# Keys and values of batches 1 and 2 laid five tokens to a partition: a cosformer attention and SwiGLU kernel on one core

## The chip, the cores and the metric

The kernel runs on one core of a Trainium2 chip. The metric is the device time of one execution in microseconds, as a median of several runs; smaller is better. A separate profiled execution gives a trace of every engine: TensorE (PE, with its weight loads shown as PEld), VectorE (DVE), ScalarE (ACT), GpSimd (POOL) and SyncE (SP, which only issues transfers). Times in the trace are counted from the start of the span.

## The reference, cut to what matters

```python
B, H, S, D = 8, 8, 576, 64                      # attention, float32
theta = pi / 2 * arange(S) / S
phi(x) = concat([relu(x) * cos(theta), relu(x) * sin(theta)], -1)     # 128 features
kv  = einsum('bhsf,bhsd->bhfd', phi(k), v)      # 128 x 64 for each head
z   = sum(phi(k), axis=2)
num = einsum('bhsf,bhfd->bhsd', phi(q), kv)
den = einsum('bhsf,bhf->bhs', phi(q), z)[..., None] + 1e-6
x   = (num / den) with heads joined             # 4608 tokens x 512
# then for every token: x / rms(x) * rms_g, and
out = (silu(xn @ w_gate) * (xn @ w_val)) @ w_out     # 512 -> 1536 -> 512
```

The sum over the 576 tokens of a head may be taken in any order. So the tokens of k and v may lie on the partitions in any way, as long as k, v and the cos and sin tables agree.

## The kernel before, in words

Most of the work is the feed-forward part: for each block of 512 tokens (one batch less its last 64 tokens; block 8 collects those tails) 12 steps `gval_step` of two products of 512x512 with 128 output features each, and then 4 steps `out_step`. The attention of the next batch is spread over these steps. Nothing is scheduled automatically: the order of the source is the order on each engine, and a table `slots` (filled by `at(block, step, where, function, ...)`, run by `run`) says in which step which small piece of attention is issued. For block 0 there is a separate opening, written out by hand (`unit_mm`, `unit_tile`, `unit_silu`, `unit_h`, and between them `nd0_pe`, `nd_post`, `x_sq`, `x_norm`, `x_tr_pe`, `x_tr_evac`).

For each batch, k and v are loaded as float32 (`load_kv`) into one of five `raw` buffers. `k_phi` (L292 on ACT, L294 on DVE) multiplies k by the cos or sin column of its token and takes the positive part, into the bfloat16 tile `kp`; `v_cast` copies v to bfloat16 with a column of ones behind each head, so that one product gives kv and z. `kvz_pe` does these products into `psA`, and `kvz_evac` copies the result out.

There are two layouts of k and v. In the narrow one (batches 0, 1 and 2) a pair of heads shares the 128 partitions, 64 each, with nine consecutive tokens of a head on each partition: 9 steps of `k_phi` with 4 x 64 elements on 128 partitions, and 9 x 8 products over 64 rows each. In the wide one (batches 3 to 7) a partition holds five consecutive tokens of all eight heads, and 116 partitions are in use: 5 steps of `k_phi` with 8 x 64 elements, and 5 x 8 products over 116 or 115 rows (the last partition holds one token). The narrow load is one transfer; the wide load is two, of 112 and of 4 partitions (L115). Batch 0 has its own code for most of this.

The loads of batches 0 to 2 and of all weights are issued by GpSimd's queue, those of batches 3 to 7 by SP's. GpSimd works in order, and besides issuing it runs small operations: the power -0.5 that ends the RMS (`rs`, L520, inside `x_sq`), which `x_norm` on VectorE reads, two `q_phi` and one `v_cast`. In the program, the transfers of GpSimd signal their ends on eight semaphores that are taken in turn, one semaphore for each transfer. GpSimd's transfers in the order of the source are, by number:

1 q of batch 0, first half (L135); 2 and 3 v of batch 0 (L213); 4 q of batch 0, second half; 5, 6, 7, 8 `wg`, `wv`, `wg`, `wv`, first eight feature blocks (L183); 9 k of batch 1 (L110); 10 `wg`, last four blocks; 11 `wv`, last four blocks; 12 q of batch 1 (L126); 13 v of batch 1 (L110); 14, 15, 16 `wo` in three parts (L189); 17 k of batch 2; 18 v of batch 2.

The part of the opening in which these lie reads, shortened:

```python
    x_sq(0, 1)
    load_q(1, eng=G)
    load_kv("v", 1, eng=G)
    ...
    x_sq(0, 2)
    load_wo(0, 4)
    ...
    x_sq(0, 3)
    load_wo(4, 8)
    load_wo(8, 12)
    unit_silu(1)
    x_norm(0, 3)
    unit_mm(2, wg)
    x_tr_pe(0, 2, psC[1])
    ...
```

with `x_tr_pe(0, 3)` after six of the eight products of `unit_mm(3, wg)`. Here `x_sq(0, j)` issues a square on ScalarE and then `rs` on GpSimd.

Of the kernel before, what the change touches and what calls it, by code (L numbers as in the profile page):

```python
# [10 lines left out]
BF16 = mybir.dt.bfloat16  # L11
# [6 lines left out]
def kernel(  # L18
# [11 lines left out]
    nc = tc.nc  # L30
    B, H, S, D = q.shape
    DM = H * D
    DFF = moe_w_gate.shape[1]
    P = 128
    TB = 512
    HP = H // 2
    NC = S // 64
    NC5 = 5
    KP = S // NC5 + 1
# [3 lines left out]
    E = D + 1  # L43
# [3 lines left out]
    V, A, G = nc.vector, nc.scalar, nc.gpsimd  # L47

    ctx.enter_context(tc.manual_schedule())
    one = ctx.enter_context(tc.tile_pool(name="one", bufs=1))  # L50
# [22 lines left out]
        )  # L73

    def wide(b):
        return b > 2

    def rows_of(c):
        return KP if c == 0 else KP - 1
# [12 lines left out]
    def raw_tile(which, b):  # L92
        if (which, b) not in raw:
            t = ring.tile([P, H * NC5 * D], FP32, name="raw", tag="raw")
            raw[(which, b)] = t
        return raw[(which, b)]

    def raw_kv(which, b):
        t = raw_tile(which, b)
        if wide(b):  # L100
            return t[:, :].rearrange("p (h e) -> p h e", h=H)
        return t[:, 0 : HP * NC * D].rearrange("p (hp e) -> p hp e", hp=HP)
# [4 lines left out]
    def load_kv(which, b, hps=(0, HP), eng=nc.sync):  # L107
        src = k if which == "k" else v
        if not wide(b):
            return eng.dma_start(  # L110
                out=raw_kv(which, b)[:, hps[0] : hps[1], :], in_=kv_rows(src, b, hps)
            )
        last = KP if b < B - 1 else KP - 1
        for r0, r1 in ((0, KM), (KM, last)):
            eng.dma_start(  # L115
                out=raw_kv(which, b)[r0:r1, :, :], in_=kv_rows5(src, b, r0, r1)
            )
        if last < KP:
            eng.dma_start(
                out=raw_kv(which, b)[last:KP, :, :].rearrange("p h (c d) -> p h c d", d=D),  # L120
                in_=src[b, :, S - 1 : S, :].rearrange("h s d -> s h d").unsqueeze(2)
                .to_broadcast([1, H, NC5, D]),
            )
# [98 lines left out]
    part, left = [], 1e-6  # L222
# [42 lines left out]
    def cos_of(c):  # L265
# [3 lines left out]
    kp = kp5[:, :, :, :].rearrange("p c h f -> p (c h f)")[:, 0 : NC * HP * F].rearrange(  # L269
        "p (c hp f) -> p c hp f", c=NC, f=F  # L270
    )
    vv = one.tile([P, HP, NC, E], BF16, name="vv")
    vv5 = one.tile([P, H, NC5, E], BF16, name="vv5")
    G.memset(vv[:, :, :, D:E], 1.0)
    G.memset(vv5[:, :, :, D:E], 1.0)
    qpT = one.tile([P, H, TB], BF16, name="qpT")
    xnT = [one.tile([P, NDT, TB], BF16, name=f"xnT{i}") for i in range(2)]
# [6 lines left out]
    def copy(eng, o, i):  # L284
        if eng is A:
            A.copy(out=o, in_=i)  # L286
        else:
            eng.tensor_copy(out=o, in_=i)  # L288

    def phi(eng, out_ap, in_ap, scale):  # L290
        if eng is A:
            A.activation(out=out_ap, in_=in_ap, func=AF.Relu, scale=scale)  # L292
        else:
            eng.tensor_scalar(  # L294
                out=out_ap, in0=in_ap, scalar1=scale, scalar2=0.0, op0=ALU.mult, op1=ALU.max
            )


    def k_phi(eng, b, c, part, hps=(0, HP)):
        o = slice(0, D) if part == 0 else slice(D, F)  # L300
        f = cos_of if part == 0 else sin_of
        if wide(b):
            rows = rows_of(c)
            src = raw_kv("k", b)[0:rows, :, c * D : (c + 1) * D]
            phi(eng, kp5[0:rows, c, :, o], src, f(14 + c)[0:rows, :])
            return
        src = raw_kv("k", b)[:, hps[0] : hps[1], c * D : (c + 1) * D]
        phi(eng, kp[:, c, hps[0] : hps[1], o], src, f(c))

    qp_tiles = {}  # L310

# [55 lines left out]
        copy(eng, qpT[:, :, j * P : (j + 1) * P], dst)  # L367

    def v_cast(eng, b, hps=(0, HP)):
        if wide(b):  # L370
            src = raw_kv("v", b).rearrange("p h (c d) -> p h c d", d=D)
            hs = slice(2 * hps[0], 2 * hps[1])
            return copy(eng, vv5[0:KP, hs, :, 0:D], src[0:KP, hs])
        copy(
            eng, vv[:, hps[0] : hps[1], :, 0:D],
            raw_kv("v", b)[:, hps[0] : hps[1], :].rearrange("p hp (c d) -> p hp c d", d=D),
        )

    heads = psA[:, :, 0 : HP * E].rearrange("p g (hp e) -> p g hp e", e=E)
    kvzs = {}  # L380

    def kvz_pe(b):
        for hp in range(HP):
            for c in range(NC5 if wide(b) else 0):
                for g in range(2):
                    h, r = 2 * hp + g, rows_of(c)
                    nc.tensor.matmul(  # L387
                        heads[:, g, hp, :], lhsT=kp5[0:r, c, h, :], rhs=vv5[0:r, h, c, :],
                        start=(c == 0), stop=(c == NC5 - 1),
                    )  # L390
            for c in range(0 if wide(b) else NC):
                for g in range(2):
                    lo, hi = 64 * g, 64 * g + 64
                    nc.tensor.matmul(  # L394
                        heads[:, g, hp, :], lhsT=kp[lo:hi, c, hp, :], rhs=vv[lo:hi, hp, c, :],
                        start=(c == 0), stop=(c == NC - 1),
                    )


# [211 lines left out]
    for c in range(NC):  # L611
        k_phi(V, 0, c, 0)
        k_phi(A if c < 8 else V, 0, c, 1)
        z0_pe(c)
        if c < NDT:
            g_spread(psC[0], c)
# [65 lines left out]
    lo, hi = (0, NDT // 2), (NDT // 2, NDT)  # L682
# [75 lines left out]
    def at(blk, n, where, f, *args):  # L758
        slots.setdefault((blk, n), {}).setdefault(where, []).append((f, args))
# [2 lines left out]
        for f, args in slots.get((blk, n), {}).get(where, []):  # L762
            f(*args)

    KCS = ((0, 1, 2), (3, 4), (5, 6), (7, 8))
    KCS5 = ((0, 1), (2,), (3,), (4,))
    for c in range(NC):
        at(0, 5 + c // 3, "post", k_phi, V, 1, c, 0)
        at(0, 5 + c // 3, "post", k_phi, A, 1, c, 1)
    for j in range(4):  # L770
        at(0, (8, 8, 9, 10)[j], "post", q_phi, V, 1, j, 0)
        at(0, 8 + j, "post", q_phi, A, 1, j, 1)
# [2 lines left out]
        at(0, 10 + j, "pre" if j < 2 else "pe", q_tr_evac, V if j < 2 else A, 1, j, bank)  # L775
    at(0, 8, "post", load_kv, "k", 2, (0, HP), G)
    at(0, 9, "post", v_cast, G, 1, (0, 2))
    at(0, 10, "post", v_cast, V, 1, (2, 4))
    at(0, 10, "post", load_kv, "v", 2, (0, HP), G)
    at(0, 12, "pe", kvz_pe, 1)  # L780
    at(0, 12, "pe", kvz_evac, A, 1)

# [21 lines left out]
    for nb in range(2, B):  # L804
        b = nb - 1
        first = nb == 2
        for i, cs in enumerate(KCS5 if wide(nb) else KCS):
            kb, kn = ((0, 14), (0, 15), (1, 0), (1, 1))[i] if first else (b - 1, 12 + i)
            for c in cs:
                at(kb, kn, "post", k_phi, V, nb, c, 0)  # L810
                at(kb, kn, "post", k_phi, A, nb, c, 1)
        for i in range(2):
            vb, vn = ((0, 15), (1, 0))[i] if first else (b - 1, 13 + 2 * i)
            at(vb, vn, "post", v_cast, V, nb, (2 * i, 2 * i + 2))
        for j in range(4):
            late = j + (nb == 3)
            qb, qn = (b, 1 + j) if first else (b - (late < 2), (14 + late) % 16)
            at(qb, qn, "post", q_phi, V, nb, j, 0)
            at(qb, qn, "post", q_phi, A, nb, j, 1)
            at(qb, qn, "post", q_tr_dma, nb, j)  # L820
        kz = 3 if first else 2
        at(b, kz, "pe", kvz_pe, nb)
        at(b, kz, "pre", kvz_evac, A, nb)
        for j in range(4):
            n = ((6, 8, 9, 11) if first else (4, 6, 8, 10))[j]
            at(b, n, "pe", nd_pe, nb, j)
            at(b, n, "pre", nd_post, nb, j)
            at(b, n, "post", x_sq, nb, j)
            m = n + 2 if first and j == 0 else n + 1
            at(b, m, "post", x_norm, nb, j)  # L830
            at(b, m, "post", x_tr_dma, nb, j)

    for pair in range(4):
        b = 2 * pair or 3
# [9 lines left out]
    for nb in range(3, B):  # L844
        b = nb - 2
# [94 lines left out]
```

## Time and profile before

| | |
|---|---|
| median of 3 runs | 323.63 us (323.45 to 323.72) |
| the profiled execution, its own time | 323.16 us |
| its span | 321.4 us |
| granted TensorE clock, mean over the span | 0.999 |
| busy PE, DVE, ACT, POOL | 317.2, 184.5, 166.2, 40.4 us |
| loads of k and v by GpSimd | 2 and 2 transfers of 1152.0 KB |
| loads of k and v by SP | 5 and 5 of 1120.0 KB, with 4 and 4 of 40.0 KB, 1 and 1 of 30.0 KB, 1 and 1 of 10.0 KB |

A group of instructions in the profile is named by line, engine, operation, the tile written and the tiles read, with the shape and the number of them. In a timeline a row gives the start, the time, the engine and line, and in brackets the idle time of the engine ahead of it with what ended it. "us to landing" of a transfer counts from its issue to the end of its last packet.

### The profile page before, as it was taken

To read this page: it belongs to the slowest core of one execution; us is meant where nothing else is said; L and a number is where in the kernel's file an instruction comes from. 1 tells how busy PE (TensorE), PEld (TensorE's weight loads), DVE (VectorE), ACT (ScalarE), POOL (GpSimd) and SP (SyncE) were. 2 spreads that over 40 slices of the span, in tenths; PEclk is the share of its full clock that TensorE was granted. 3 is DMA by queue.
4 is the path that set the end of the run, shared out by engine and by line. 5 is a ranking of instruction groups with operands and counts; after the bars stand their busy time and mean duration, and the time that the engine had idled before them with its cause. 6 is when DMAs were issued, how large, how long until landed. Compare 5 with 4: busy or idle time off the path is not lost.

```text
span 321.4 us, 6061 instructions
## 1 busy us (share of the span) xinstructions
PE 317.2 (99%) x2310; PEld 162.5 (51%) x2310; DVE 184.5 (57%) x382; ACT 166.2 (52%) x322; POOL 40.4 (13%) x79
## 2 busy tenths in 40 slices
PE   8999999999999999999999999999999999999996
PEld 2689564554454445444544445544544444444444
DVE  7976858668447773777457645781676034204410
ACT  5766756754584466554744575446543333223321
POOL 9771211002001100011001100100011000000000
PEclk9999999999999999999999999999999999999999
DMA  7999999987999989999799859995522500041002
GB/s 234 238 274 268 279 330 159 262 183 189 227 224 203 194 260 189 234 250 168 159 190 230 195 161 200 198 217 162 99 58 42 116 33 0 0 102 31 1 35 98
DMA packets 80091, 53.76 MB, mean 167 GB/s; under 512 B 52234, under 2 KB 74046, under 8 KB 80062
## 3 DMA queue, kind: packets, MB, share of 16 engines
q1 hardware_dynamic: 73110, 41.25, 62.0%
q0 software_dynamic: 6944, 12.13, 15.5%
q8 instruction: 18, 0.29, 0.4%
q14 instruction: 11, 0.09, 0.1%
q10 hardware_dynamic: 8, 0.00, 0.0%
HBM read 37.83 MB, written 9.44 MB: 147 GB/s over the span
## 4 chain that ended last, share of the span: by engine, by line
PE 97%; DVE 1%; ACT 0%; issue 0%; POOL 0%; ACTq 0%
PE psC L579 27%; PE psG L556 27%; PE psV L556 27%; PE psA L449 2%; PE psV L648 2%; PE psG L579 2%; PE psG L648 2%; PE psA L387 2%; PE psC L603 1%; PE psC L410 1%; PE psA L394 1%; PE psA L474 0%; PE psV L363 0%; PE psG L430 0%; PE psC L546 0%; PE psC L233 0%
## 5 line engine op out<-in xcount | busy, mean ns | idle before, releaser
L576 DVE TENSOR_TENSOR hT<-psV,sg 128x512 bf16<-128x512 f32 x100 | 68.9, 689 | 97.7 <-PE psV L556 65.4
L575 ACT ACTIVATE sg<-psG 128x512 f32<-128x512 f32 x100 | 59.2, 592 | 62.3 <-PE psG L556 61.0
L556 PE MATMUL psV<-xnT,wv 128*128 128x512 bf16 x352 | 90.3, 379 | 0.0
L556 PE MATMUL psG<-xnT,wg 128*128 128x512 bf16 x352 | 90.3, 379 | 0.0
L579 PE MATMUL psC<-wo,hT 128*128 128x512 bf16 (+1 forms) x408 | 88.9, 376 | 0.0
L579 PEld LDWEIGHTS <-hT 128*128 128x128 bf16 x456 | 43.0, 98 | 47.8
L556 PEld LDWEIGHTS <-wv 128*128 128x128 bf16 x400 | 39.1, 98 | 47.2
L556 PEld LDWEIGHTS <-wg 128*128 128x128 bf16 x400 | 36.9, 98 | 39.8 <-DVE xnT L288 0.4
L520 POOL TENSOR_TENSOR rs<-ms,mhalf 128x1 f32<-128x1 f32 x36 | 20.5, 571 | 194.6 <-ACT scr L515 194.4
L286 ACT COPY osb<-psC 128x512 f32<-128x512 f32 x32 | 18.8, 586 | 49.9 <-PE psC L579 49.9
L515 ACT ACTIVATE scr<-xt 128x513 bf16<-128x513 f32 x36 | 22.8, 634 | 25.1 <-DVE xt L499 24.4
L527 DVE SCALAR_TENSOR_TENSOR xn<-xt,rs,gb 128x512 bf16<-128x512 f32 (+1 forms) x37 | 27.0, 731 | 9.9 <-POOL rs L520 9.8
L292 ACT ACTIVATE kp<-raw,tab 128x256 bf16<-128x256 f32 (+2 forms) x51 | 28.8, 607 | 2.2 <-DMA raw<-in_k_dram 2.2
L499 DVE TENSOR_TENSOR xt<-psA,rec 128x512 f32<-128x512 f32 x36 | 24.9, 691 | 1.2
L292 ACT ACTIVATE qp<-raw,tab 128x512 bf16<-128x512 f32 (+1 forms) x36 | 23.4, 666 | 1.0 <-DMA raw<-in_q_dram 0.8
L294 DVE TENSOR_SCALAR kp<-raw,tab 128x256 bf16<-128x256 f32 (+2 forms) x53 | 19.9, 423 | 0.5 <-DMA raw<-in_k_dram 0.5
L294 DVE TENSOR_SCALAR qp<-raw,tab 128x512 bf16<-128x512 f32 (+1 forms) x34 | 15.4, 466 | 4.2 <-DMA raw<-in_q_dram 4.2
L449 PEld LDWEIGHTS <-qpT 128*128 128x128 bf16 x224 | 10.5, 97 | 6.7 <-issue 0.7
L556 PE MATMUL psV<-xnT_tail,wv 128*128 128x512 bf16 x48 | 12.3, 379 | 0.0
L556 PE MATMUL psG<-xnT_tail,wg 128*128 128x512 bf16 x48 | 12.3, 379 | 0.0
L449 PE MATMUL psA<-kvzs,qpT 128*128 128x65 bf16 x224 | 11.4, 193 | 0.0
L288 DVE CAST vv<-raw 116x1280 bf16<-116x1280 f32 (+1 forms) x13 | 10.5, 807 | 1.1 <-DMA raw<-in_v_dram 1.1
(100 smaller groups left out, 178.2 us busy)
## 6 DMA issues: line engine op xcount, KB each, us to landing
out_dram<-osb SPq DMA_DIRECT2D x27, 256.0 KB, 2.3
raw<-in_q_dram SPq DMA_DIRECT2D x6, 1024.0 KB, 9.3
raw<-in_k_dram SPq DMA_DIRECT2D x5, 1120.0 KB, 8.5
raw<-in_v_dram SPq DMA_DIRECT2D x5, 1120.0 KB, 9.5
raw<-in_k_dram POOLq DMA_DIRECT2D x2, 1152.0 KB, 19.4
raw<-in_v_dram POOLq DMA_DIRECT2D x2, 1152.0 KB, 16.0
out_dram<-osb SPq DMA_DIRECT2D x17, 128.0 KB, 2.7
wg<-in_moe_w_gate_dram POOLq DMA_DIRECT2D x3, 512.0 KB, 13.6
```

The costliest lines, as they stand in the source:

```text
L286: A.copy(out=o, in_=i)
L292: A.activation(out=out_ap, in_=in_ap, func=AF.Relu, scale=scale)
L294: eng.tensor_scalar(out=out_ap, in0=in_ap, scalar1=scale, scalar2=0.0, op0=ALU.mult, op1=ALU.max)
L449: nc.tensor.matmul(heads[:, g, hp, :], lhsT=qpT[:, h, j * P : (j + 1) * P], rhs=kvzs[b][:, g, hp * E : (hp + 1) * E], start=True, stop=True,)
L499: V.tensor_tensor(out=xt[:, 0:DM].rearrange("p (hp g d) -> p g hp d", g=2, d=D), in0=heads[:, :, :, 0:D], in1=rec[:, :, :].unsqueeze(3).to ...
L515: A.activation(out=scr[:, :], in_=xt[:, 0 : DM + 1], func=AF.Square, scale=1.0 / math.sqrt(DM), accum_out=ms[:, :],)
L520: G.tensor_tensor(out=rs[:, :], in0=ms[:, :], in1=mhalf[:, :], op=ALU.pow)
L527: V.scalar_tensor_tensor(out=xn_of[(b, j)][:, c], in0=x_of[(b, j)][:, c], scalar=rs_of[(b, j)][:, :], in1=gb[:, c], op0=ALU.mult, op1=ALU. ...
L556: nc.tensor.matmul(bank[:, cols[0] : cols[1]], lhsT=w[:, t, n * P : (n + 1) * P], rhs=x[:, t, cols[0] : cols[1]], start=(t == 0), stop=(t ...
L575: A.activation(out=sg[:, :], in_=g[:, 0:TB], func=AF.Silu)
L576: V.tensor_tensor(out=hT[:, n, :], in0=v[:, 0:TB], in1=sg[:, :], op=ALU.mult)
L579: nc.tensor.matmul(bank[:, 0 : cols[1] - cols[0]], lhsT=hT[:, n, j * P : (j + 1) * P], rhs=wo[:, n, cols[0] : cols[1]], start=(n == 0), st ...
```

## The change

Batches 1 and 2 take the wide layout too: `wide(b)` is true from batch 1 on. With it the tile `vv` of the narrow layout and its memset go, and so do the narrow branches of `v_cast` and `kvz_pe`; the steps of `k_phi` of batch 1 in block 0 and of batch 2 become five instead of nine. `load_kv` for batches 1 and 2 issues two transfers on GpSimd's queue where it issued one, at the same places in the source. The order of everything else stays.

```diff
     def wide(b):
-        return b > 2
+        return b > 0
...
-    vv = one.tile([P, HP, NC, E], BF16, name="vv")
     vv5 = one.tile([P, H, NC5, E], BF16, name="vv5")
-    G.memset(vv[:, :, :, D:E], 1.0)
...
-        src = raw_kv("k", b)[:, hps[0] : hps[1], c * D : (c + 1) * D]
-        phi(eng, kp[:, c, hps[0] : hps[1], o], src, f(c))
+        phi(eng, kp[:, c, :, o], raw_kv("k", b)[:, :, c * D : (c + 1) * D], f(c))
...
     def v_cast(eng, b, hps=(0, HP)):
-        if wide(b):
-            src = raw_kv("v", b).rearrange("p h (c d) -> p h c d", d=D)
-            hs = slice(2 * hps[0], 2 * hps[1])
-            return copy(eng, vv5[0:KP, hs, :, 0:D], src[0:KP, hs])
-        copy(
-            eng, vv[:, hps[0] : hps[1], :, 0:D],
-            raw_kv("v", b)[:, hps[0] : hps[1], :].rearrange("p hp (c d) -> p hp c d", d=D),
-        )
+        src = raw_kv("v", b).rearrange("p h (c d) -> p h c d", d=D)
+        hs = slice(2 * hps[0], 2 * hps[1])
+        copy(eng, vv5[0:KP, hs, :, 0:D], src[0:KP, hs])
...
-            for c in range(NC5 if wide(b) else 0):
+            for c in range(NC5):
...
-            for c in range(0 if wide(b) else NC):
-                for g in range(2):
-                    lo, hi = 64 * g, 64 * g + 64
-                    nc.tensor.matmul(
-                        heads[:, g, hp, :], lhsT=kp[lo:hi, c, hp, :], rhs=vv[lo:hi, hp, c, :],
-                        start=(c == 0), stop=(c == NC - 1),
-                    )
...
-    KCS = ((0, 1, 2), (3, 4), (5, 6), (7, 8))
     KCS5 = ((0, 1), (2,), (3,), (4,))
-    for c in range(NC):
-        at(0, 5 + c // 3, "post", k_phi, V, 1, c, 0)
-        at(0, 5 + c // 3, "post", k_phi, A, 1, c, 1)
+    for c in range(NC5):
+        at(0, 5 + c // 2, "post", k_phi, V, 1, c, 0)
+        at(0, 5 + c // 2, "post", k_phi, A, 1, c, 1)
...
-        for i, cs in enumerate(KCS5 if wide(nb) else KCS):
+        for i, cs in enumerate(KCS5):
```

More of the change, by code (lines that the diff above doesn't have):

```diff
@@ L296, in phi, with k_phi @@
             )
-    def k_phi(eng, b, c, part, hps=(0, HP)):
+    def k_phi(eng, b, c, part):
         o = slice(0, D) if part == 0 else slice(D, F)
```

## The prediction

> **What bounds the kernel now.** I read the page first, its busy times and the chain that ended last.
>
> ```profile
> PE 317.2 (99%) x2310; PEld 162.5 (51%) x2310; DVE 184.5 (57%) x382; ACT 166.2 (52%) x322; POOL 40.4 (13%) x79
> ...
> PE 97%; DVE 1%; ACT 0%; issue 0%; POOL 0%; ACTq 0%
> ```
>
> TensorE sets the end: 97% of the chain is products, one behind the other. So an edit counts only if it changes the products or makes TensorE wait. The chain in order of time has the products that change, as pieces (start, length):
>
> ```profile
> 59.58 1.27 PE psA L394 x72
> ...
> 91.36 1.23 PE psA L387 x40
> ```
>
> L394 is the narrow form, L387 the wide one. The 72 products over 64 rows cost hardly more than 40 over 116, so their count promises nothing.
>
> What else the change touches is GpSimd's queue, so next I read its timeline around the loads.
>
> ```profile
> 15.73 0.82 POOL L183 DMA_DIRECT2D wv<-in_moe_w_val_dram  x1
> 16.68 0.56 POOL L520 TENSOR_TENSOR rs<-ms,mhalf 128x1 f32<-128x1 f32 x1
> 17.21 0.94 POOL L126 DMA_DIRECT2D raw<-in_q_dram  x1
> 18.15 0.77 POOL L110 DMA_DIRECT2D raw<-in_v_dram  x1
> 19.80 0.56 POOL L520 TENSOR_TENSOR rs<-ms,mhalf 128x1 f32<-128x1 f32 x1 [0.89 <-ACT scr L515]
> 20.32 0.79 POOL L189 DMA_DIRECT2D wo<-in_moe_w_out_dram  x1
> 21.56 0.56 POOL L520 TENSOR_TENSOR rs<-ms,mhalf 128x1 f32<-128x1 f32 x1 [0.45 <-ACT scr L515]
> 22.09 0.79 POOL L189 DMA_DIRECT2D wo<-in_moe_w_out_dram  x1
> 23.47 0.74 POOL L189 DMA_DIRECT2D wo<-in_moe_w_out_dram  x1 [0.60 <-DMA wv<-in_moe_w_val_dram]
> 26.69 0.76 POOL L110 DMA_DIRECT2D raw<-in_k_dram  x1 [2.48 <-DMA raw<-in_k_dram]
> ```
>
> Two rows matter. The third wo load waits for a wv load whose data it does not touch, and k of batch 2 waits for k of batch 1, whose buffer is another one. By number they are transfer 16, which waits for 8, and 17, which waits for 9: a transfer waits until the one eight before it has landed, for its semaphore. The landing times of 7 (issued 6.65), 8 (7.45) and 9 (8.97), each the last number of its row:
>
> ```profile
> wg<-in_moe_w_gate_dram POOLq DMA_DIRECT2D x1, 512.0 KB, 13.6
> ...
> wv<-in_moe_w_val_dram POOLq DMA_DIRECT2D x1, 512.0 KB, 15.7
> ...
> raw<-in_k_dram POOLq DMA_DIRECT2D x1, 1152.0 KB, 17.2
> ```
>
> They land at 20.25, 23.15 and 26.17, and the waits above end at 23.47 and 26.69, 0.32 and 0.52 later. Before the change, both waits stand behind the last rs of the opening, so nobody waits for them.
>
> Last, who reads rs: VectorE's norm, then TensorE's transposes.
>
> ```profile
> 20.55 0.74 DVE L527 SCALAR_TENSOR_TENSOR xn<-xt,rs,gb 128x512 bf16<-128x512 f32 x1
> 22.16 0.75 DVE L527 SCALAR_TENSOR_TENSOR xn<-xt,rs,gb 128x512 bf16<-128x512 f32 x1 [0.87 <-POOL rs L520]
> ```
>
> ```profile
> 22.18 0.39 PE L546 MATMUL psC<-ident,xn 128*128 128x128 bf16 x4
> 22.40 0.82 PE L648 MATMUL psG<-xnT,wg 128*128 128x256 bf16 x6
> 23.05 0.39 PE L546 MATMUL psC<-ident,xn 128*128 128x128 bf16 x4
> ```
>
> The norm of tile 3 ends at 22.91 and its transposes run at 23.05: rs of tile 3 has almost no slack to TensorE.
>
> **The change part by part.**
>
> *Products.* Twice 1.27 us becomes twice 1.23: 0.08 us saved on the path.
>
> *ScalarE, VectorE, casts.* k of batch 1 costs ACT three pieces of 1.29 and DVE three of 0.87 (3.87 and 2.61). Batch 3, wide, costs ACT 1.33 and three of 0.72, DVE 1.27 and 0.88 (3.49 and 2.15). A half of the v cast goes from 0.74 to 0.83 on DVE; GpSimd's half, 1.15 for 1152 columns, to about 1.28 for 1280 by size. All of it lies beside products: nothing on the path. One memset (0.27) leaves GpSimd.
>
> *Transfers, time of the data.* A load becomes 928 runs of 1280 B in place of 512 of 2304 B, with 1160 KB for 1152. In the queue's order wv lands at 31.0, q of batch 1 at 34.1 (1024 runs of 1024 B in 3.1 us) and v at 37.05 (512 of 2304 B in 2.95). Over 16 DMA engines that is 48 and 92 ns a run, by a line 57 ns for 1280 B: an estimate of 58 x 57 ns = 3.3 us, 0.35 more. If the four last rows run on four engines only, 8 more runs, 0.45 us, come on top. Bounds: 0 (bytes alone) to 0.8 us a load; I take 0.4, nearest the line. Who would feel it: q of batch 1 has 0.8 us (its first ACT step ends at 34.88, the transposes start at 35.70) against one load; k and v of batch 2 have 3.7 and 4.2 us (landed 48.3 and 51.25, used at 51.99 and 55.45) against four. The tightest is the second wo part, landed at 42.1 and used at about 42.7, with two loads ahead of it: 0.6 us of cover against 0.8. Bare, that would cost 0.2 us (0 to 1.0); with TensorE later by the next step it costs nothing.
>
> *Transfers, their issue.* Four more issues of about 0.76 us, and every number behind them moves. The new count: 9 and 10 k of batch 1, 11 wg, 12 wv, 13 q, 14 and 15 v of batch 1, 16 to 18 wo, 19 and 20, 21 and 22 the loads of batch 2. Then:
>
> - 10 waits for 2 (landed 9.5), 11 for 3 (3.75 + 7.3 = 11.05): GpSimd issues wg at about 11.35, its memset ends near 12.5, and its two q steps start at 12.68 as before, since that is when ACT releases them (1.62 us idle there).
> - 15, the four rows of v, waits for 7 (20.25): issue at 20.57, end at 21.31. Queued behind it is rs of tile 2, which moves from 19.80 to 21.31.
> - 16, the first wo part, waits for 8 (23.15), as transfer 16 does now: it starts at the same 23.47 and ends at 24.21. Queued behind it is rs of tile 3, which moves from 21.56 to 24.21: 2.65 us.
>
> VectorE's norm of tile 3 started 0.60 after rs did, so it starts at 24.81 and ends at 25.56; the transposes of tile 3 go from 23.05 to about 25.7. Those of tile 2, pushed from 22.18 to 22.7, are inside this. On VectorE the norm is ahead of the copy of tile 2's transposes and of the first two products with silu, and all go along. What follows needs TensorE's own results; the largest of the later waits of TensorE's weight loads is 0.43 us, at 54.21, for a tile made on this same chain. So I see nothing to take the 2.65 back. Later issues (17 waits for 9, 18 for 10, 19 for 11, 20 for 12) keep GpSimd busy waiting until about 32, with transfers queued for the DMA engines all that time and no rs before 45.72. Bounds for the step: release 0.1 to 0.5 (0.32 as seen), issue 0.7 to 0.94: 2.35 to 3.05.
>
> *Sum.* 323.16, the profiled execution's own time (span 321.4 and 1.76 around it), less 0.08, plus 2.65, gives 325.73. The median of the runs stands 0.47 above that execution: 326.2. With the bounds, 325.7 to 326.8.
>
> **The rivals.**
>
> *The clock drops in the gap.* TensorE would idle from about 23.5 to 25.7, after 0.5 us shortly before. [...]
>
> ```profile
> 1.18 4.45 PE L603 MATMUL psC<-warm 128*128 128x512 bf16 x10 [1.18 <-DVE warm L164]
> ```
>
> 445 ns a product, against 216 later (four in 0.86). If 2.2 us of idling brought this back for as long, half of 4.45 would be lost: 326.2 + 2.2 = 328.4, with up to 0.5 more. For it: two gaps close together, with little work between them. Against it: the trace shows no drop after a short gap, but it has no gap of this length either (0.84 us before 5.55 is the longest). [...] I give this rival 0.11.
>
> *No wait from the count, so not slower.* If waits 16 for 8 and 17 for 9 have another reason, or the small transfers do not take a number of their own, GpSimd issues four rows of v at 18.92, ends by 19.7, and rs of tile 2 still starts at 19.80. Then only the products (-0.08) and the 0.2 us at wo are left, or neither: 323.55 to 323.75, up to 324.5 at the bound of the loads. What decides is whether rs of tile 3 starts by 21.7. Against it: two waits at a distance of exactly eight, on tiles that share no data. 0.11, with 0.07 of it within 0.2%.
>
> *A gain beyond 0.2%.* Some 0.65 us would have to come from work on the path, and only 0.08 us of that shrinks. 0.03.
>
> *Something larger*, such as a second wait of TensorE for data behind the delayed issues: over 329. 0.03. My sum keeps 0.72.
>
> **How the numbers follow.** 0.2% (0.65 us) is about what a measurement of this kernel tells from no change. The likeliest case is 326.2. Its own range, widened for run to run, is 325.3 to 327.1; reaching up to the clock rival takes in 0.83: 325.3 to 328.9. Slower: 0.72 + 0.11 + 0.03 and 0.03 from the second rival, 0.89. Same: 0.07. Faster: 0.03 and 0.01 from the second rival, 0.04.
>
> **What would show it.** GpSimd's timeline after: a load of v waiting for a wg load until about 20.6, the first wo part at 23.5 waiting for wv, rs of tile 3 near 24.2. TensorE: a wait of some 2 us ahead of L546 that ends near 25.7, charged to VectorE's norm; products of 128x512 with four in 0.86 us right behind it (if near 1.7, the clock rival). The 40 products at 1.23 us for batches 1 and 2. If rs of tile 3 starts before 22, the count of eight is wrong and with it the forecast; if the gap is there but the end is not 2.6 later, then something later had slack that I did not see.

## The result and the profile after

The change makes the kernel slower: 332.43 us median (330.75 to 334.37, 6 runs) against 323.74 us (323.45 to 323.87, 6 runs), a ratio of 1.0273 with a 95% interval of 1.0252 to 1.0295. The forecast was 326.2 us, with a range of 325.3 to 328.9. The sign was right, the size, 2.5 us, was under a third of the 8.7 that came. The spread is new as well: 0.4 us before, 3.6 us after.

The page of the profiled execution after (332.98 us, span 331.2), its busy times and the chain that ended last:

```profile
PE 316.7 (96%) x2210; PEld 162.9 (49%) x2246; DVE 184.5 (56%) x374; ACT 165.0 (50%) x314; POOL 43.9 (13%) x82
...
PE 81%; DMA 14%; POOL 2%; DVE 2%; issue 1%; POOLq 0%
```

TensorE's busy time has not grown. But transfers, absent from the chain before, now hold 14% of it. GpSimd's timeline around the loads shows the forecast mechanism:

```profile
18.61 0.84 POOL L115 DMA_DIRECT2D raw<-in_v_dram  x1
21.02 0.62 POOL L115 DMA_DIRECT2D raw<-in_v_dram  x1 [1.57 <-DMA wg<-in_moe_w_gate_dram]
21.66 0.56 POOL L505 TENSOR_TENSOR rs<-ms,mhalf 128x1 f32<-128x1 f32 x1
23.69 0.81 POOL L189 DMA_DIRECT2D wo<-in_moe_w_out_dram  x1 [1.47 <-DMA wv<-in_moe_w_val_dram]
24.52 0.56 POOL L505 TENSOR_TENSOR rs<-ms,mhalf 128x1 f32<-128x1 f32 x1
28.90 1.54 POOL L189 DMA_DIRECT2D wo<-in_moe_w_out_dram  x2 [3.82 <-DMA raw<-in_k_dram]
```

The four rows of v wait for wg until 21.02 (forecast 20.57), the first wo part waits for wv until 23.69 (23.47), and rs of tile 3 runs at 24.52 (24.21). It goes on to TensorE, whose timeline has the transposes of tile 3 at 25.93 instead of 23.05 (forecast about 25.7):

```profile
23.30 0.82 PE L633 MATMUL psG<-xnT,wg 128*128 128x256 bf16 x6
25.93 0.40 PE L531 MATMUL psC<-ident,xn 128*128 128x128 bf16 x4 [1.81 <-DVE xn L512]
```

Up to here the forecast holds. TensorE's waits in the whole span then show what it did not have:

```profile
PE psG L541 <- DMA xnT<-xn: 2.9, 1, 2.9
PE psC L531 <- DVE xn L512: 2.1, 2, 1.8
PE psA L379 <- POOL vv L286: 1.7, 1, 1.7
...
PE psC L360 <- ACT qp L290: 0.3, 1, 0.3
...
PE psG L564 <- DMA wo<-in_moe_w_out_dram: 0.2, 1, 0.2
```

L531 is the step above. L360, L379 and L564 wait for q, v and wo, each landed late; L541 is the start of block 1, which waits for the transposed xn (`xnT`, written by transfers on SP's queue). Not all of the 1.7 us at L379 is the transfer of v. GpSimd's half of the v cast, before and after:

```profile
37.15 1.15 POOL L288 CAST vv<-raw 128x1152 bf16<-128x1152 f32 x1 [9.71 <-DMA raw<-in_v_dram]
...
43.74 1.90 POOL L286 CAST vv<-raw 116x1280 bf16<-116x1280 f32 x1 [9.73 <-DMA raw<-in_v_dram]
```

The same cast of 1280 columns takes 1.25 us in `e_128`, `e_128all`, `e_best`, `e_data`, `e_b1` and `e_b2`, where VectorE's half comes later, and 1.90 or 1.91 in the three traces in which VectorE's half starts within 0.05 us of it (this one at 43.70, `e_112only` and `e_fill`). So some 0.65 us of the wait goes with the overlap of the two casts; no run changes that overlap alone.

Behind the wait at block 1 the granted clock falls. In stretches of 2 us (busy time of PE, PEld, DVE, ACT and POOL, then PEclk, the DMA share and GB/s):

```profile
60.00:62.00 2.00, 0.00 (x0) 0.00 (x0) 1.48 (x3) 0.02 (x1) 0.00 (x0) 1.00 1.06 189
62.00:64.00 2.00, 1.45 (x5) 0.62 (x6) 0.12 (x1) 0.00 (x0) 0.00 (x0) 0.76 1.09 329
64.00:66.00 2.00, 2.00 (x5) 0.71 (x5) 0.22 (x1) 1.21 (x2) 0.00 (x0) 0.50 1.09 382
66.00:68.00 2.00, 1.78 (x9) 0.88 (x9) 1.65 (x4) 0.98 (x2) 0.00 (x0) 0.89 0.76 284
```

So TensorE's lateness against the trace of before grows like this, each number a difference of the start of the same products in the two timelines:

| place | before | after | late by | grown by |
|---|---|---|---|---|
| second half of the k-v products of batch 0 | 11.51 | 12.05 | 0.5 | 0.5 |
| transposes of tile 3 | 23.05 | 25.93 | 2.9 | 2.3 |
| first transposes of q of batch 1 | 35.70 | 39.04 | 3.3 | 0.5 |
| k-v products of batch 1 | 40.59 | 45.69 | 5.1 | 1.8 |
| first products of block 1 | 54.24 | 62.55 | 8.3 | 3.2 |
| its second step, wv | 56.83 | 66.82 | 10.0 | 1.7 |
| end of the span | 321.4 | 331.2 | 9.8 | -0.2 |

The first row is a v load of batch 0 that lands at 11.57 in place of 11.05. It is issued ahead of everything that changed, and the other kernels below have it at 10.8 to 11.8 (`e_data` apart): variation of that execution.

What makes the data late is the time that a load takes. From issue to landing, v of batch 1 before and after, then k of batch 1 after:

```profile
raw<-in_v_dram POOLq DMA_DIRECT2D x1, 1152.0 KB, 18.9
...
raw<-in_v_dram POOLq DMA_DIRECT2D x1, 1120.0 KB, 24.8
...
raw<-in_k_dram POOLq DMA_DIRECT2D x1, 1120.0 KB, 19.6
```

In the queue's order k lands at 28.61, 5.2 us behind the wv ahead of it (23.40), and v 5.2 us behind q (38.24 to 43.44). Before, both took 3.0. The packet records of the trace say the same: GpSimd's queue packed two runs of 2304 B into 4608 B, median 192 ns; now it packs four runs of 1280 B into 5120 B, median 360 ns.

### The profile page after: what moved, and what is told of

Read it like the earlier page. It is cut to its first block, busy times and chain, and to the rows that moved or that the text cites. A ratio compares the mean times of both kernels' runs of the same rounds, so it can differ in the third digit from the quotient of the medians.

```text
span 331.2 us, 5891 instructions
## 1 busy us (share of the span) xinstructions
PE 316.7 (96%) x2210; PEld 162.9 (49%) x2246; DVE 184.5 (56%) x374; ACT 165.0 (50%) x314; POOL 43.9 (13%) x82
## 4 chain that ended last, share of the span: by engine, by line
PE 81%; DMA 14%; POOL 2%; DVE 2%; issue 1%; POOLq 0%
PE psV L541 25%; PE psG L541 25%; PE psC L564 25%; DMA raw<-in_k_dram 6%; DMA wo<-in_moe_w_out_dram 6%; PE psA L379 2%; PE psA L434 2%; DMA xnT<-xn 2%; PE psG L564 1%; DVE xt L484 1%; DVE xn L512 1%; POOL raw L135 1%; POOL wg L183 0%; PE psA L459 0%; POOL wv L183 0%
## 5 line engine op out<-in xcount | busy, mean ns | idle before, releaser
L541 PE MATMUL psG<-xnT,wg 128*128 128x512 bf16 x337 | 89.3, 381 | 3.7 <-DMA xnT<-xn 2.9
L541 PE MATMUL psV<-xnT,wv 128*128 128x512 bf16 x345 | 90.7, 382 | 0.6
L564 PE MATMUL psC<-wo,hT 128*128 128x512 bf16 (+1 forms) x399 | 88.5, 376 | 0.5
L564 PEld LDWEIGHTS <-hT 128*128 128x128 bf16 x456 | 43.0, 98 | 48.1 <-issue 0.4
L541 PEld LDWEIGHTS <-wv 128*128 128x128 bf16 x400 | 39.3, 98 | 47.8 <-issue 1.1
L541 PEld LDWEIGHTS <-wg 128*128 128x128 bf16 x400 | 37.1, 98 | 43.2 <-DVE vv L286 3.4
L290 ACT ACTIVATE kp<-raw,tab 115x512 bf16<-115x512 f32 (+2 forms) x43 | 27.8, 678 | 2.2 <-DMA raw<-in_k_dram 2.2
L292 DVE TENSOR_SCALAR kp<-raw,tab 115x512 bf16<-115x512 f32 (+2 forms) x45 | 19.2, 466 | 0.5 <-DMA raw<-in_k_dram 0.5
L541 PE MATMUL psV<-xnT_tail,wv 128*128 128x512 bf16 x48 | 12.3, 379 | 0.1
L286 DVE CAST vv<-raw 116x1280 bf16<-116x1280 f32 x13 | 10.7, 823 | 2.6 <-DMA raw<-in_v_dram 2.6
L541 PE MATMUL psG<-xnT_tail,wg 128*128 128x512 bf16 x46 | 12.0, 379 | 0.1
```

The lines of the kernel that those rows point to most:

```text
L292: eng.tensor_scalar(out=out_ap, in0=in_ap, scalar1=scale, scalar2=0.0, op0=ALU.mult, op1=ALU.max)
L541: nc.tensor.matmul(bank[:, cols[0] : cols[1]], lhsT=w[:, t, n * P : (n + 1) * P], rhs=x[:, t, cols[0] : cols[1]], start=(t == 0), stop=(t ...
L564: nc.tensor.matmul(bank[:, 0 : cols[1] - cols[0]], lhsT=hT[:, n, j * P : (j + 1) * P], rhs=wo[:, n, cols[0] : cols[1]], start=(n == 0), st ...
```

## The experiments

### The numbers alone, and the partition count

`e_slots` keeps the narrow layout and only doubles the number of transfers:

```diff
         if not wide(b):
-            return eng.dma_start(
-                out=raw_kv(which, b)[:, hps[0] : hps[1], :], in_=kv_rows(src, b, hps)
-            )
+            for hp in range(hps[0], hps[1], 2):
+                eng.dma_start(
+                    out=raw_kv(which, b)[:, hp : hp + 2, :], in_=kv_rows(src, b, (hp, hp + 2))
+                )
+            return
```

> The kernel before, narrow layout everywhere, but each of the four k and v loads of batches 1 and 2 goes out on GpSimd's queue as two transfers (two head pairs each), so the transfers are numbered as in the changed kernel while runs (2304 B) and bytes stay. Theory of the prediction (a transfer waits for the one eight before it): rs of tile 3 moves from 21.6 to about 24.3, TensorE waits some 2.5 us before the transposes of tile 3, and the time is 326.2 to 326.8. Rival (the loss lies in the data of the wide loads, the numbers do not matter): 323.5 to 324.2.

Measured: 327.35 us (326.51 to 329.9), ratio 1.0134, interval 1.009 to 1.0179. Packets stay at 191 ns. GpSimd's timeline has the same wait, and TensorE's the gap behind it:

```profile
21.17 0.72 POOL L111 DMA_DIRECT2D raw<-in_v_dram  x1 [1.68 <-DMA wg<-in_moe_w_gate_dram]
...
25.02 0.80 POOL L191 DMA_DIRECT2D wo<-in_moe_w_out_dram  x1 [2.55 <-DMA wv<-in_moe_w_val_dram]
25.84 0.57 POOL L522 TENSOR_TENSOR rs<-ms,mhalf 128x1 f32<-128x1 f32 x1
```

```profile
27.25 0.61 PE L548 MATMUL psC<-ident,xn 128*128 128x128 bf16 x4 [2.88 <-DVE xn L529]
```

So the count of eight is shown, without the wide layout. The two runs with a granted clock of 1.0 took 326.51 and 326.9, at the upper end of what was expected; the others, at 0.995 and 0.99, took 327.79 and 329.9, and so the median is above what was expected. Against the 323.28 of the kernel before in the same set, the first two are 3.2 and 3.6 us slower, more than the forecast 2.65. The profiled run is the one of 329.9. Its clock fell inside that gap: the stretch from 26 us is at 0.50 throughout, and the transposes start at 27.25.

```profile
26.00:28.00 2.00, 0.74 (x6) 0.69 (x7) 1.55 (x3) 0.10 (x1) 1.23 (x3) 0.50 1.23 212
28.00:30.00 2.00, 2.00 (x15) 1.63 (x14) 0.73 (x2) 0.98 (x2) 0.72 (x1) 0.50 1.21 264
```

`e_128` keeps the wide layout and loads all 128 partitions in one transfer:

```diff
-        for r0, r1 in ((0, KM), (KM, last)):
+        for r0, r1 in ((0, P),) if b < 3 else ((0, KM), (KM, last)):
```

> The changed kernel, but k and v of batches 1 and 2 are loaded by one transfer of all 128 partitions each (the last twelve rows are not used): 18 transfers as before, runs of 1280 B, 1280 KB. Theory C (112 partitions are what makes the packets slow, 360 ns for 5120 B): packets near 210 ns, 3.4 us a load, time 323.5 to 325. Theory D (runs of 1280 B, four to a packet, are slow on GpSimd's queue): packets near 360 ns, 5.8 us a load, time 331 to 335.

Measured: 323.74 us (323.32 to 324.12), ratio 1.0011, interval 1.0002 to 1.0021. Packets of the same 5120 B: 229 ns. A load takes 3.5 us in the queue's order (23.20 to 26.69, 34.86 to 38.38), with 160 KB more than the transfer of 112 partitions. Of the change's loss 0.46 us is left here (323.74 against 323.28; `e_128all` and `e_best` below, with the same loads of batches 1 and 2, show none). TensorE's waits in its profile:

```profile
PE psG L415 <- DMA vv<-in_v_dram: 0.8, 1, 0.8
PE psG L564 <- DMA wo<-in_moe_w_out_dram: 0.4, 1, 0.4
```

The first is v of batch 0 again, which the change does not touch. The second is the second wo part, the tightest row of the prediction: landed at 43.31, against 42.04 before.

`e_nar112` is the cross-check, narrow runs with 112 + 16 partitions:

```diff
-            return eng.dma_start(
-                out=raw_kv(which, b)[:, hps[0] : hps[1], :], in_=kv_rows(src, b, hps)
-            )
+            for r0, r1 in ((0, KM), (KM, P)):
+                eng.dma_start(
+                    out=raw_kv(which, b)[r0:r1, :, :], in_=kv_rows(src, b, hps)[r0:r1, :, :]
+                )
+            return
```

> The kernel before, narrow layout, but each k and v load of batches 1 and 2 goes out as two transfers of 112 and 16 partitions: runs of 2304 B, numbers as in the changed kernel. Theory C (112 partitions make the packets slow): packets of 4608 B near 330 ns instead of 192, about 4.7 us a load, time 329 to 333. Theory D (the run length does it): packets near 192 ns, only the waits by number remain, 326.2 to 326.8.

Measured: 332.89 us (330.25 to 334.58), ratio 1.0285, interval 1.0233 to 1.0338. It is as slow as the change, with none of its layout. Packets of 4608 B: 307 ns against 192. Theory C holds on both sides: what slowed the data in these runs is how many partitions one transfer covers (360 ns against 229 for 5120 B, 307 against 192 for 4608 B), and not the runs of 1280 B.

`e_parts` takes other cuts, for the packets alone:

```diff
...
+            cut = {("k", 1): 96, ("v", 1): 64, ("k", 2): 120, ("v", 2): 80}.get((which, b), KM)
-            for r0, r1 in ((0, KM), (KM, P)):
+            for r0, r1 in ((0, cut), (cut, P)):
...
```

> One look, for the packets alone: the kernel before (narrow, runs of 2304 B, two to a packet of 4608 B), with each load of batches 1 and 2 cut into two transfers at another partition: k of batch 1 at 96 (96 + 32), v of batch 1 at 64 (64 + 64), k of batch 2 at 120 (120 + 8), v of batch 2 at 80 (80 + 48). Theory C1 (only transfers in which all 16 engines have eight partitions run at 190 ns): every piece is at 280 ns or more. Theory C2 (a share of partitions that is a power of two is enough): 64 + 64 at 190, 96, 80 and 120 at 280 or more. Theory C3 (112 alone is bad): 96 and 80 at 190.

Measured, in its one execution (336.93 us): packets of 333 and 329 ns (medians of 2 us stretches with more than 30 packets) while k of batch 1 came in as 96 + 32, 339 to 368 while v came as 64 + 64, 301 to 460 through 120 + 8 and 80 + 48. None ran near 190 but at the very start of a load (178 at 20 to 22 us, 185 at 46 to 48). The times are those that C1 expected, 280 ns or more, as far as a stretch tells, since the two pieces of a load are not told apart in it. Its reason, eight partitions to each of 16 engines, is not shown: no run tells which engine writes which partition. Why these cuts are slow at all is left open.

### Late data without the waits by number

`e_data` moves only the four-row transfers to SP's queue:

```diff
-            eng.dma_start(
+            (nc.sync if r0 else eng).dma_start(
```

> The changed kernel, but the four-row transfers of batches 1 and 2 go out on SP's queue, so GpSimd has 18 transfers numbered as before and none of the new waits ahead of rs. Theory A (the data of the wide loads is slow on GpSimd's queue, landing at 28.6 and 43.4 for k and v of batch 1, and this sets the k-v products at about 45.7 whatever GpSimd did before): rs of tile 3 back at 21.6, but the time stays at 331 to 333. Theory B (the losses add up): 2.4 to 2.9 less than the changed kernel, 329.5 to 330.

Measured: 334.04 us (333.62 to 335.07), ratio 1.0334, interval 1.0308 to 1.036. That is outside both ranges, and the experiment does not tell the theories apart. SP issues the rows of k and v of batch 1 at 1.77 to 2.5 us; v of batch 0 then landed at 14.94 against 11.05, and TensorE was late before the loads in question landed. The next experiment does without SP:

`e_112only` leaves the four-row transfers out, and with them the last 16 tokens of each head of batches 1 and 2:

```diff
-    def rows_of(c):
+    def rows_of(c, b=B):
+        if b < 3:
+            return KM
...
-        for r0, r1 in ((0, KM), (KM, last)):
+        for r0, r1 in ((0, KM),) if b < 3 else ((0, KM), (KM, last)):
...
```

> The changed kernel without the four-row transfers of batches 1 and 2: their k and v use 112 partitions only, and the last 16 tokens of each head are left out of kv and z. GpSimd has 18 transfers, numbered as before, and SP issues nothing extra. It has the slow data of 112 partitions without the new waits by number. Theory A (late data sets the k-v products of batch 1 whatever GpSimd did before): rs of tile 3 at 21.6 to 22, no wait before the transposes of tile 3, v of batch 1 lands near 43, its products run near 45, time 330 to 332.5. Theory B (the losses add up): v of batch 1 lands near 43 but the time is 2.4 to 2.9 below the changed kernel, 329.5 to 330.

Measured: 329.0 us (327.95 to 332.02), ratio 1.0183, interval 1.0131 to 1.0236. TensorE's waits in its profile:

```profile
PE psC L362 <- ACT qp L292: 1.9, 1, 1.9
PE psG L544 <- DVE kp L294: 1.2, 1, 1.2
...
PE psA L382 <- POOL vv L288: 1.0, 1, 1.0
PE psG L567 <- DMA wo<-in_moe_w_out_dram: 0.5, 1, 0.5
```

The wait for xn of tile 3 is gone, and 4.6 us of waits come in its place, for q, v, wo and at block 1. The late data alone costs about 5 us. Both theories missed in part: v landed at 41.72, its products ran at 43.73 and not at 45, so the median came out below both ranges, nearer to B. The two causes add up more than I had thought, 329.0 with the one and 332.43 with both.

### Batch 1 and batch 2 apart

`e_b2` has the slow transfers for batch 2 alone, `e_b1` for batch 1 alone; the other batch has one transfer of 128 partitions. Shown for `e_b2`; `e_b1` has `b == 2`.

```diff
-        for r0, r1 in ((0, KM), (KM, last)):
+        for r0, r1 in ((0, P),) if b == 1 else ((0, KM), (KM, last)):
```

> The changed kernel with batch 1 loaded by one transfer of 128 partitions each; only batch 2 keeps 112 + 4. No new wait ahead of rs, and TensorE is on time up to out_first. Theory E (v of batch 2, still on its way, makes the transposed xn of block 1 land late, and the wait of about 3 us lets the clock fall): v of batch 2 lands near 57, xnT takes about 6 us in place of 3.3, TensorE waits 2 to 3 us before block 1, some granted clock of 0.5 behind it, time 326.5 to 328.5. Rival F (the late xnT of the changed kernel came from the shifts ahead of it): no such wait, 323.5 to 324.3.

Measured: 328.68 us (326.31 to 329.15), ratio 1.0144, interval 1.0104 to 1.0183. TensorE is on time up to the k-v products of batch 1 (40.45). Then v of batch 2 lands at 56.46 and, from TensorE's timeline and the stretches behind it:

```profile
58.13 1.42 PE L541 MATMUL psG<-xnT,wg 128*128 128x512 bf16 x4 [3.27 <-DMA xnT<-xn]
```

```profile
58.00:60.00 2.00, 1.87 (x6) 0.76 (x7) 0.00 (x0) 0.42 (x1) 0.00 (x0) 0.66 1.10 350
60.00:62.00 2.00, 1.78 (x5) 0.69 (x5) 0.65 (x2) 0.78 (x2) 0.00 (x0) 0.50 1.07 388
62.00:64.00 2.00, 2.00 (x10) 0.92 (x10) 1.64 (x4) 1.40 (x3) 0.00 (x0) 0.99 0.57 205
```

Theory E holds, though the median is 0.2 us above its range. The loads of batch 2 by themselves make the transposes late (6.6 us to landing against 3.3 before), and the clock falls behind the wait.

> The changed kernel with batch 2 loaded by one transfer of 128 partitions each; only batch 1 keeps 112 + 4. The waits by number ahead of rs are there, and v of batch 1 lands near 43. Theory E (k and v of batch 1 cost some 5 us at the k-v products; what comes at xnT is batch 2's): the k-v products of batch 1 run near 45.5, v of batch 2 lands near 57, which leaves a wait at xnT of 0 to 2 us, time 328.5 to 331. Rival F (the wait at xnT follows from batch 1 alone): as the changed kernel, 331 to 333.

Measured: 328.37 us (327.65 to 328.97), ratio 1.0152, interval 1.0125 to 1.0179. That is 0.1 us below the range of Theory E. In its profile there is no wait at block 1: what comes there in the changed kernel is batch 2's. The k-v products of batch 1 ran at 45.66 as expected, but for another reason. TensorE's gap ahead of tile 3 was 2.91 us, the granted clock was 0.83, 0.50 and 0.82 in the three stretches from 26 to 32, and TensorE was then so late that v (landed 43.25) no longer made it wait.

### The clock

`e_fill` puts products of zeros into the gap:

```diff
     out_first()
+    filler(10, psV[0])
```

> The changed kernel with ten products of zeros (512 columns, about 2.2 us) on TensorE between out_first and block 1, in the gap where it waits for xnT. Theory G (the idle gap of 2.9 us is what lets the clock fall to half for some 4 us): no granted clock under 0.9 after the gap, the first twelve products of block 1 at four in 0.87 us, 1.3 to 1.7 us less than the changed kernel, 330.5 to 331.2. Rival H (the clock falls for another reason, or the products take the place of waiting only): the same 0.5 stretch, 331.5 to 334.

Measured: 331.2 us (329.62 to 332.11), ratio 1.0231, interval 1.0197 to 1.0264. The stretches of its profile:

```profile
62.00:64.00 2.00, 1.95 (x10) 0.88 (x10) 0.56 (x1) 0.24 (x1) 0.00 (x0) 1.00 1.09 331
64.00:66.00 2.00, 2.00 (x11) 0.94 (x10) 1.30 (x3) 1.48 (x4) 0.00 (x0) 1.00 1.12 384
```

Block 1 starts at 62.70, as late as in the changed kernel (62.55), but the clock stays up and the second step with wv follows 2.6 us later instead of 4.3. That fits Theory G. It is not the whole of it, though. `e_nar112` waits at the same place without a filler, and its clock stays at 1.00:

```profile
61.31 1.02 PE L558 MATMUL psG<-xnT,wg 128*128 128x512 bf16 x4 [2.77 <-DMA xnT<-xn]
```

```profile
60.00:62.00 2.00, 0.69 (x4) 0.36 (x5) 0.47 (x1) 0.00 (x0) 0.00 (x0) 1.00 1.15 315
62.00:64.00 2.00, 2.00 (x11) 0.94 (x10) 0.69 (x2) 1.39 (x3) 0.00 (x0) 1.00 1.09 357
```

So behind a wait of 2.90 us the clock fell, and behind one of 2.77 it did not. Of the six runs of the changed kernel one kept a clock of 1.0 (331.56 us); of the four of `e_fill` one was at 0.995, and it was the fastest (329.62). The median of `e_fill` is 1.2 us below that of the changed kernel, but the two intervals overlap: a gain in time is not shown.

### SP's queue, and a better version

`e_128all` uses one transfer of 128 partitions up to batch 6:

```diff
-        for r0, r1 in ((0, P),) if b < 3 else ((0, KM), (KM, last)):
+        for r0, r1 in ((0, P),) if b < B - 1 else ((0, KM), (KM, last)):
```

> One transfer of 128 partitions for k and v of batches 1 to 6 (batch 7 as before), so the loads that SP issues change as well. Theory I (the partition count slows the transfers of SP's queue too, where packets of 1280 B rise from 55 to 90 ns): the packets of SP's k load near 68 to 74 us stay at 55 to 60 ns. Rival J (SP's queue has another cause): they rise to 80 to 100 as before. The time is not set by these loads in either case: 323.3 to 324.

Measured: 323.39 us (323.29 to 323.8), ratio 1.0002, interval 0.9993 to 1.0012. The packets of 1280 B have a median of 55 ns in each of the stretches from 69 to 74 us; in the trace of before they rise to 81, 78 and 91. Theory I holds: the slowness is not GpSimd's. The stretch of SP's k load, first before, then in `e_128all`:

```profile
69.50:73.00 3.50, 3.50 (x31) 1.80 (x30) 2.75 (x6) 1.48 (x4) 0.41 (x1) 1.00 1.08 290
...
69.50:73.00 3.50, 3.45 (x30) 1.81 (x30) 2.15 (x6) 1.76 (x4) 0.55 (x1) 1.00 0.95 327
```

`e_best` is `e_128` with the wo part that TensorE waits for cut in two:

```diff
-    load_wo(4, 8)
+    load_wo(4, 6)
+    load_wo(6, 8)
```

> The one-transfer kernel of 128 partitions for batches 1 and 2, with the second part of wo (four blocks) cut into two of two blocks, so that the block which TensorE waits for lands earlier. The wait of 0.4 us before the fifth product with wo goes; the new 19 transfers put no wait ahead of rs. Theory: 323.1 to 323.5, as the kernel before or 0.1 us below it. Rival (the 0.4 us is given back at another transfer): 323.6 to 324.

Measured: 323.57 us (323.28 to 323.93), ratio 1.0001, interval 0.9992 to 1.0009. That is between the two ranges expected. The wait at wo is gone; in its profile TensorE waits 0.8 us at the start of block 1 instead, so the Rival (the 0.4 us is given back elsewhere) is not ruled out. In the median the wide layout costs nothing any more. It gains nothing either: the 0.08 us on the products is less than a measurement tells. No version here beats the kernel before.

## Why the prediction was right in part, and wrong in size

- *Transfers, their issue*: right in mechanism, and near in size for this trace. Forecast 2.65 us; the trace has 2.3 (2.9 less the 0.5 of the start). The closeness is partly luck. The step hangs on the landing of wv, which I took from one trace (23.15), and which came at 23.13 to 24.73 in the six traces with the doubled numbers; the transposes of tile 3 started at 25.64 to 27.25 in them, against 25.7, and `e_slots` lost 3.2 to 3.6 us with the full clock. My bounds, 2.35 to 3.05, were too narrow.
- *Transfers, time of the data*: this term failed. I took 0.4 us more for a load, with bounds of 0 to 0.8, from two loads of 128 partitions with other runs. It is 2.2 us (5.2 against 3.0). That the four last rows run on four engines, 0.45 us of the upper bound, was an assumption that no run shows. The variable that mattered here, the number of partitions (360 ns for a packet of 5120 B with 112, 229 with 128), was not in my line at all. With it failed "it costs nothing". The cover of q, 0.8 us, was too small, and TensorE waited 0.3 us for it. My list of who would feel it had no cover for v of batch 1 (a wait of 1.7 us, some 0.65 of it the overlapping casts, where I had priced GpSimd's half at 1.28 and it took 1.90). And it left out the transposes of xn, which ran while loads of batch 2 were under way. In this row the landing time is that of the last transpose, first before, then after:

```profile
xnT<-xn SPq DMA_TRANSPOSE x3, 3.3
...
xnT<-xn SPq DMA_TRANSPOSE x3, 6.2
```

Before, it was issued at 50.81 and landed at 54.1, with block 1 starting on it at 54.24: no cover to speak of. After, it was issued at 56.17 and landed at 62.4, and block 1 started at 62.55.

A row that would have warned me was in the trace of before. SP's own load of 112 partitions, in its stretch from 69.5 to 73 us, ran at 290 GB/s with the DMA share at 1.08 (the row is shown above), where the end of the narrow queue had 409, the last figure of this row of before:

```profile
44.00:46.00 2.00, 2.00 (x24) 1.28 (x22) 1.15 (x4) 1.09 (x3) 0.28 (x1) 1.00 1.04 409
```

By it, a load of 1120 KB would be some 4.0 us: an estimate, 1.0 us more than before, so a warning and not yet the 5.2. And `e_128all`, with all 128 partitions, moves 327 in that stretch, so part of the distance to 409 is not the partition count. I priced the new transfer by the wrong relatives, while the kernel had ten loads of the very form.

- *The clock drops in the gap*: I gave it 0.11, for the gap ahead of tile 3. In the profiled run it did not fall there (1.81 us) but behind the wait at block 1 (2.90 us), where it cost 1.7 us (I had priced such a fall at 2.2). That price was an estimate from the 445 ns of the first products. The granted clock reads 1.00 there (the stretches from 0 to 6 us of the trace of before), so they do not show a fallen clock; behind the wait at block 1, at 0.50, four products took 1.71 us, 428 ns each. My sum kept the full clock through a gap of 2.2 us, which no trace had shown either. In `e_slots`, `e_b1` and `e_nar112` the clock fell at the gap that I meant (2.88, 2.91 and 2.40 us); at 1.81 us, and at 2.25 in `e_fill`, it stayed at 1.00. So it belonged in the sum of the likeliest case as a cost that some runs have.
- *No wait from the count*: refuted by `e_slots`.
- *A second wait for data*: named with 0.03 as "something larger", behind the delayed issues. The waits came, but not because of the delayed issues: `e_112only` has them without those.
- *What would show it*: the last sentence of that part came true in its mirror image. The gap was there and the end was later than 2.6 us, because something had less slack than I saw.

## What to carry to other kernels

Price a new transfer by one of the same form in the trace, above all of the same number of partitions, and look at its rate in a stretch where it is alone. List everybody who waits for a transfer near it, the transfers of other queues too. Count what the queue's completion semaphores allow: here the split of four loads moved the waits behind it, and a small operation that shares the queue paid for it (rs of tile 3 at 24.52 instead of 21.56). This kernel, with TensorE at 99%, had little slack for late data (329.0 us with them alone against 323.75, `e_112only`), and in five profiled kernels (the changed one, `e_slots`, `e_nar112`, `e_b1`, `e_b2`) a granted clock of 0.50 came in or behind a stall of 2.40 to 3.27 us, for 1.7 us more in the changed one.

## What the runs showed of the hardware that I had not expected

- A transfer of 112 partitions took 5.2 us for 1120 KB (k and v of batch 1, in the queue's order), one of 128 partitions 3.5 us for 1280 KB (`e_128`); cuts at 64, 80, 96 and 120 are slow too (301 to 460 ns a packet against 192). On SP's queue packets of 1280 B went from 55 to some 80 or 90 ns. q of batch 1, of 128 partitions itself, took 5.1 us in the changed kernel against 3.1 (its packets at 292 and 333 ns in the stretches from 34 and 36 us, in which packets of v were under way too).
- Two casts from one buffer, on GpSimd and on VectorE, were longer when they ran together: GpSimd's 1.90 us instead of 1.25 where VectorE's began first, and in `e_parts`, where GpSimd's began first (44.09, 1.15 us), VectorE's 1.71 us instead of 0.76.
- The granted clock fell to 0.50 in idle gaps, or within 1.2 us behind them, of 2.40 (`e_nar112`), 2.53 and 2.98 (`e_data`), 2.54 and 4.72 (`e_parts`), 2.88 (`e_slots`), 2.90 (the changed kernel), 2.91 (`e_b1`) and 3.27 us (`e_b2`). It did not at 1.81 (the changed kernel, ahead of tile 3), at 2.25 (`e_fill`, ahead of tile 3), nor at 2.77 (`e_nar112`, block 1), so the length alone does not decide. Summed over the stretches, as if the clock were always at 1.00 or at 0.50, it stayed low for 3.4 us in the changed kernel, `e_b1`, `e_b2` and `e_nar112`, and for 6.8 in `e_slots`: an estimate from the PEclk of the 2 us stretches. Why it falls at one gap and not at another is left open.
